# Attention loop of a block kernel: stack rows of maxima in halves, lead 18, six fixed score banks, split output copies

## The chip, the cores and the metric

The kernel runs on one core of a Trainium2 chip. A core has five engines with queues of their own: PE (TensorE, the matmuls, whose weight loads the profile lists apart as PEld), DVE (VectorE), ACT (ScalarE), POOL (GpSimd) and SP (SyncE, which issues most DMAs here). PE writes its results into PSUM, in banks of 128 partitions by 512 float32 values; DVE and ACT read them from there. Operands lie in SBUF, and what moves between SBUF and DRAM moves by DMA. The metric is the device time of one execution in microseconds (us), given as the median of several runs.

## The reference

The reference computes one block in float32 for S = 2048 tokens of width D = 640: attention over 32 heads of width 20 in which a token sees itself and the 255 tokens before it, then a gated MLP whose gate mixes tokens with a matrix of 2048 x 2048.

```python
def _A_ref(x, wqkv, wo):
    H = 32; Dh = D // H; W = 256
    q, k, v = ...                                   # x @ wqkv, by heads
    scores = jnp.einsum("bhqd,bhkd->bhqk", q, k) * (Dh ** -0.5)
    mask = (idx[:, None] - idx[None, :] >= 0) & (idx[:, None] - idx[None, :] < W)
    p = _softmax(jnp.where(mask, scores, -1e9), axis=-1)
    return jnp.einsum("bhqk,bhkd->bhqd", p, v).reshape(B, S, D) @ wo

def _B_ref(x, w_in, w_sp, b_sp, w_out):
    z = _gelu(jnp.einsum("bsd,df->bsf", x, w_in))
    z1, z2 = z[..., :Fh], _layernorm(z[..., Fh:], axis=-1)
    g = jnp.einsum("ts,bsf->btf", w_sp, z2) + b_sp[None, :, None]
    return jnp.einsum("bsf,fd->bsd", z1 * g, w_out)

h = x + _A_ref(_layernorm(x), A_wqkv, A_wo)
h2 = h + _B_ref(_layernorm(h), B_w_in, B_w_sp, B_b_sp, B_w_out)
```

## The kernel before

**Stages.** Up to some 85 us the kernel normalises x, transposes it and forms the values (turn1, vgemm). Then it forms queries and keys by 40 gemm items (qk_item), each of which is split into three bf16 parts (split_qk: ACT copies the first part, DVE takes the rest, ACT copies the second part, POOL takes the third) and stored to qk_d in DRAM. The last 16 of these items, cut into 80 steps of three matmuls by the generator dense_tail, are interleaved with the first maxima of the attention. From 249 to some 499 us the attention loop runs. The rest, to the end, is the output projection, the second layernorm and the MLP.

**Tiling of the attention.** There are eight groups of four heads and 16 key blocks of 128 tokens, in all NU = 128 units; a unit is one key block of one group. A stack of a group (a slot, of which three rotate: tiles slot0, slot1 and xb, each in two halves of 1024 tokens) holds the bf16 parts of queries and keys as rows 0 to 119, and as query rows 120 to 122 the negated maximum of each query in three bf16 parts. So the score matmul over 123 rows gives the score less its maximum, and ACT need only take the exponential. A stack is loaded by load_stack in DMAs on SP.

**One turn of the loop** (`for s in range(NU + 2)`) issues, four times, a maximum for unit s + LEAD and a score for unit s, and between them the two parts of the value product for unit s - 2:

- max_item: four column strips of 32 queries (L298; L302 in the prologue, where the tile is not cut into strips) into a PSUM bank, and a DVE operation (L307, "junk") that adds the mask and takes the maximum over keys into one column of mcol; its result comes out by an accumulator read, which the profile lists as an instruction of its own.
- score_item: four strips (L360) into a bank, then the exp on ACT (L362) into the tile pt, and after the fourth head one or two affine selects on POOL (L364, L367), which set masked values to zero.
- pv_item: the value products in float32 (L385) into PSUM, in the first part after the second score and in the second part after the fourth. After every fourth key block the sum goes to SBUF (tile ot, on ACT at L396 or DVE at L398) and to o_d by a DMA.
- max_rows, once per group, after the last maximum of a group: PE transposes mcol (L312), DVE splits the negated maxima into three bf16 parts (L315 to L319, tiles m3 and mr), one DMA stores them to m_d (L320) and two bring them into the rows 120 to 122 of the two halves of the stack (L323).

LEAD is 21. Before the loop, the prologue issues 16 units of group 0 with three gemm steps a unit, max_rows(0), and five units of group 1, of which the last has only its four maxima.

**PSUM.** Two banks are for the value products and the gemms (pv_tile). Three rotating tiles of one bank each are for maxima (s1_tile), and three fixed tiles of one bank each for scores (s2_tile); the layernorm stage uses s2_tile for the transposes of turn1 and s1_tile for the second half of vgemm. When the last unit's maxima are issued, at s = 107, the pool is opened again as three tiles of two banks, and the last 20 units are scored two heads at a time (width 2): unstripped, with one exp for both.

**What sets the order.** Up to the end of the attention the order on PE, DVE and ACT is the order in which the code emits the instructions; a planner places what SP and POOL do, and the work of the later stages. Which semaphore an instruction waits for is not written in the kernel: it is derived from the tiles that it reads and writes.

Of the kernel before, what the change touches and what calls it, by code (L numbers as in the profile page):

```python
# [7 lines left out]
F32 = mybir.dt.float32  # L8
# [26 lines left out]
def block_kernel(ctx, tc, x, wqk, wv, wo, w_in, wsp, bsp, w_out, out):  # L35
# [5 lines left out]
    def pool(stack, name, **kw):  # L41
        return stack.enter_context(tc.tile_pool(name=name, bufs=1, reuse_waits="tile", **kw))
# [156 lines left out]
    with ExitStack() as ab:  # L199
# [38 lines left out]
        psB = ab.enter_context(ExitStack())  # L238
        ps6 = [pool(psB, "ps6", space=PSUM)]
# [44 lines left out]
        def max_item(g, qb, hh, strips=True):  # L284

            st = slot_ap[g % 3]
            ps = s1_tile(f"sm{g}_{qb}_{hh}")
            lo = max(0, qb - 2) * P
            n = (qb + 1) * P - lo
            keep = mask[:, 384 - n:]  # L290
            if strips:
                skip = 32 if qb > 1 else 0
                if skip:
                    n, keep = 288, strip
                for j in range(4):
                    q0 = qb * P + 32 * j
                    for o, w, k in tokens(st, 120, 1, hh, lo + skip * j, n):
                        nc.tensor.matmul(ps[32 * j:32 * j + 32, o:o + w], one(st, 120, 0, hh, q0, 32), k,  # L298
                                         start=True, stop=True, tile_position=(0, 32 * j))
            else:  # L300
                for o, w, k in tokens(st, 120, 1, hh, lo, n):
                    nc.tensor.matmul(ps[:, o:o + w], one(st, 120, 0, hh, qb * P, P), k, start=True, stop=True)  # L302
            if qb == 0 and hh == 0:
                m_cols[g] = tmp2.tile([P, 64], F32, tag="mcol", bufs=2, name=f"mcol{g}")
            junk = tmp2.tile([P, 384], BF16, tag="junk", bufs=2, name=f"junk{g}_{qb}_{hh}")
            c = qb // 8 * 32 + hh * 8 + qb % 8
            nc.vector.tensor_tensor_reduce(out=junk[:, :n], in0=ps[:, :n], in1=keep, scale=1.0,  # L307
                                           scalar=NEG, op0=OP.add, op1=OP.max, accum_out=m_cols[g][:, c:c + 1])

        def max_rows(g):  # L310
            ps = s1_tile(f"mt{g}")
            nc.tensor.transpose(ps[:64, :P], m_cols.pop(g), ident)  # L312
            m3 = tmp2.tile([64, 3, P], BF16, tag="m3", bufs=1, name=f"m3_{g}")
            mr = tmp2.tile([64, P], F32, tag="mr", bufs=2, name=f"mr{g}")
            nc.vector.tensor_scalar(out=m3[:, 0], in0=ps[:64, :P], scalar1=-1.0, scalar2=None, op0=OP.mult)  # L315
            nc.vector.scalar_tensor_tensor(out=mr, in0=ps[:64, :P], scalar=-1.0, in1=m3[:, 0],
                                           op0=OP.mult, op1=OP.subtract)
            nc.vector.tensor_copy(out=m3[:, 1], in_=mr)
            nc.vector.tensor_tensor(out=m3[:, 2], in0=mr, in1=m3[:, 1], op=OP.subtract)  # L319
# [19 lines left out]
            yield  # L339


        def score_item(u, hh, width):
# [8 lines left out]
            if width == 1:  # L351
                ps = s2_tile(f"st{u}_{hh}")[:, None, :]
            else:
                ps = ps6[0].tile([P, 2, 512], F32, tag="sp", bufs=3, name=f"st{u}_{hh}")
            for j in range(width):
                for i in range(4):
                    k0 = kb * P + 32 * i
                    b, e = (32 * i, min(n, 32 * i + 288)) if width == 1 else (0, n)
                    for o, w, q in tokens(st, 123, 0, hh + j, kb * P + b, e - b):
                        nc.tensor.matmul(ps[32 * i:32 * i + 32, j, b + o:b + o + w], one(st, 123, 1, hh + j, k0, 32), q,  # L360
                                         start=True, stop=True, tile_position=(0, 32 * i))
            nc.scalar.activation(pt[:, hh:hh + width, :n], ps[:, :, :n], AF.Exp, scale=SCALE)  # L362
            if hh + width == 4:
                nc.gpsimd.affine_select(out=pt[:, :, :P], in_=pt[:, :, :P], pattern=[[0, 4], [1, P]], base=0,  # L364
                                        channel_multiplier=-1, compare_op=OP.is_ge, fill=0.0)
                if n == 384:
                    nc.gpsimd.affine_select(out=pt[:, :, 256:], in_=pt[:, :, 256:], pattern=[[0, 4], [-1, P]],  # L367
                                            base=-1, channel_multiplier=1, compare_op=OP.is_ge, fill=0.0)

        def pv_item(u):  # L370
# [20 lines left out]
            if kb % 4 == 3:  # L391
                c = kb // 4
                ps = pv_tiles.pop((g, c))
                ot = tmp3.tile([P, 512], F32, tag="ot", bufs=4, name=f"ot{g}_{c}")
                if u < NU - LEAD or u >= NU - 5:
                    nc.scalar.activation(ot, ps, AF.Copy)  # L396
                else:
                    nc.vector.tensor_copy(out=ot, in_=ps)  # L398
                nc.sync.dma_start(o_d[4 * g:4 * g + 4, :, c * 512:(c + 1) * 512].rearrange("h d t -> (h d) t"), ot)
                if g == 7:  # L400
                    inverse.append(inverse_sums(c))


        if True:
# [13 lines left out]
            def turn1(i):  # L418
                xn = xns.pop(i)
                c, o = divmod(i, 4)  # L420
                for k0, k1 in ((0, 4), (4, KD)):
                    ps = s2_tile(f"xt_ps{i}_{k0}")
# [8 lines left out]
            def vgemm(i):  # L431
                c, o = divmod(i, 4)
                t0 = o * P
                for j in range(2):
                    ps = (s1_tile if j else pv_tile)(f"v{i}_{j}")
# [145 lines left out]
        for s in range(NU + 2):  # L581
# [603 lines left out]
```

## Time and profile before

| | us |
|---|---|
| median of 3 runs | 1173.26 (1172.56 to 1174.24) |
| the profiled execution | 1168.04 |
| its span | 1166.4 |
| attention loop: first exp to last exp | 252.9 to some 491 |
| mean granted TensorE clock | 0.988 |

Busy time of the engines by stage (us; the last column is the granted clock):

| stage | span | PE | DVE | ACT | POOL | clock |
|---|---|---|---|---|---|---|
| layernorm, transposes, values, 0 to 85 | 85.0 | 76.2 | 42.9 | 31.5 | 22.0 | 1.00 |
| query and key gemms, 91 to 189 | 98.0 | 97.5 | 18.7 | 39.3 | 45.3 | 1.00 |
| gemms with maxima, 189 to 249 | 60.0 | 58.1 | 48.3 | 15.3 | 21.5 | 0.99 |
| attention loop, 249 to 500 | 251.0 | 225.0 | 204.6 | 210.4 | 157.2 | 0.97 |
| projection and MLP, 500 to the end | 666.4 | 638.0 | 434.4 | 240.1 | 145.7 | 0.99 |

In the profile's rows a line number is followed by the engine, the operation and the tiles, output before inputs, without buffer numbers. A share of busy time is a mean over the stretch that it is taken from. Successive matmuls overlap in the records, so a matmul's own duration is longer than its share of PE's order; the distance between starts tells the latter. In brackets at the end of a timeline row stands how long the engine was idle before, and what ended that.

### The profile page before, as it was taken

Reading aid. Unit: us, or ns where it says so; the run is one execution under the profiler, and the core shown is the slowest. Engines: PE = TensorE matmul, PEld = TensorE weight load, DVE = VectorE, ACT = ScalarE, POOL = GpSimd, SP = SyncE. Lnnn points to the kernel's source line nnn. Section 1 sums busy time; section 2 is a strip of 40 time slices with the busy share of each in tenths; the row PEclk is TensorE's granted clock in tenths of the full one; section 3 lists DMA queues with packets and bytes.
Section 4 is the critical chain, followed back from the end, with each engine's and each line's share of the span. In section 5 each row is a group of like instructions: output and inputs, shape, how many; then the busy total and the mean of one; then the engine's idle time right before and its main releaser. Section 6 shows DMA issues by size and latency. Waiting matters only on the chain. (4 is left out here: it accounts for less than half of the span.)

```text
span 1166.4 us, 28287 instructions
## 1 busy us (share of the span) xinstructions
PE 1100.8 (94%) x11084; PEld 983.9 (84%) x11084; DVE 748.8 (64%) x1950; ACT 538.5 (46%) x1122; POOL 394.0 (34%) x480
## 2 busy tenths in 40 slices
PE   6999999989898999888999998999999899999998
PEld 6998877657777776577999997899999799999998
DVE  5541214878888895679858579655548984655443
ACT  4334433248888898634346544433334431222110
POOL 3124443436565666756412055000116430000000
PEclk9999999989999999999999999999999999999999
DMA  6212454654445523567745511233341454444322
GB/s 205 68 40 86 160 188 148 223 188 162 162 168 168 174 94 99 197 210 263 257 151 207 176 66 55 78 113 112 118 140 63 141 184 136 142 134 141 91 84 79
DMA packets 75061, 165.32 MB, mean 142 GB/s; under 512 B 10112, under 2 KB 34432, under 8 KB 71040
## 3 DMA queue, kind: packets, MB, share of 16 engines
q1 hardware_dynamic: 72624, 158.28, 40.6%
q10 hardware_dynamic: 2304, 5.24, 1.2%
q8 instruction: 87, 1.43, 0.5%
q14 instruction: 46, 0.38, 0.1%
HBM read 108.83 MB, written 54.66 MB: 140 GB/s over the span
## 5 line engine op out<-in xcount | busy, mean ns | idle before, releaser
L362 ACT ACTIVATE pt<-s 128x384 f32<-128x384 f32 (+2 forms) x432 | 171.8, 496 | 22.2 <-PE sm L298 13.7
L650 ACT ACTIVATE aw<-fx 128x512 fp32r<-128x512 f32 (+2 forms) x160 | 92.9, 596 | 188.9 <-PE g L982 121.9
L982 PE MATMUL g<-zl,aw 128*128 128x432 f32 x768 | 172.6, 360 | 7.4 <-ACT zl L650 4.9
L307 DVE CUSTOM_DVE_ANT_0 junk<-sm,strip 128x288 bf16<-128x288 f32 x380 | 153.9, 454 | 20.6 <-PE sm L298 17.1
L982 PEld LDWEIGHTS g<-zl,aw 128*128 128x128 f32 x768 | 143.9, 188 | 15.2 <-ACT zl L650 5.7
L982 PE MATMUL g<-ze,aw 128*128 128x432 f32 x576 | 137.0, 365 | 5.3 <-DVE row L644 3.1
L644 DVE TENSOR_TENSOR aw<-fx,aw 128x512 fp32r<-128x512 f32 (+2 forms) x152 | 109.8, 730 | 36.0 <-ACT aw L650 31.2
L385 PE MATMUL pv<-pt,v_sb 128*32 128x192 f32 (+3 forms) x1984 | 128.7, 323 | 4.2 <-POOL pt L364 2.5
L982 PEld LDWEIGHTS g<-ze,aw 128*128 128x128 f32 x576 | 108.9, 192 | 12.7 <-DVE row L644 2.8
L364 POOL TENSOR_SCALAR_AFFINE_SELECT pt<-pt 128x512 f32<-128x512 f32 x128 | 85.5, 668 | 82.4 <-ACT pt L362 82.2
L1021 PE MATMUL out_ps<-wout,y_sp 128*128 128x320 f32 (+1 forms) x630 | 96.4, 309 | 0.5 <-ACT y_sp L122 0.4
L360 PE MATMUL s<-slot 123*32 123x288 bf16 (+5 forms) x1216 | 88.7, 280 | 8.1 <-DMA slot<-m_d 4.2
L1021 PEld LDWEIGHTS out_ps<-wout,y_sp 128*128 128x128 f32 (+1 forms) x630 | 94.1, 188 | 1.5 <-ACT y_sp L122 0.7
L886 PE MATMUL zb<-win,aw 128*128 128x432 f32 x480 | 95.3, 359 | 0.0
L886 PEld LDWEIGHTS zb<-win,aw 128*128 128x128 f32 x480 | 90.0, 187 | 4.7
L298 PE MATMUL sm<-slot 120*32 120x288 bf16 (+8 forms) x1200 | 86.5, 280 | 2.2 <-DVE mcol L307 1.6
L480 DVE TENSOR_TENSOR rest<-qk,sg 128x512 f32<-128x512 f32 x40 | 27.7, 691 | 86.5 <-ACT sg L478 86.5
L360 PEld LDWEIGHTS <-slot 123*32 123x32 bf16 x1728 | 59.3, 97 | 25.6 <-issue 8.5
L483 POOL TENSOR_TENSOR sg<-rest,sg 128x512 bf16<-128x512 f32 x40 | 46.6, 1165 | 81.2 <-ACT sg L482 77.1
L367 POOL TENSOR_SCALAR_AFFINE_SELECT pt<-pt 128x512 f32<-128x512 f32 x112 | 72.9, 651 | 0.0
L385 PEld LDWEIGHTS pv<-pt,v_sb 128*32 128x32 f32 x1984 | 59.7, 110 | 14.0 <-POOL pt L364 6.7
L644 DVE TENSOR_TENSOR row<-g,row 128x432 f32<-128x432 f32 x80 | 47.9, 603 | 35.7 <-PE g L982 32.8
(181 smaller groups left out, 2245.0 us busy)
## 6 DMA issues: line engine op xcount, KB each, us to landing
slot<-qk_d SPq DMA_DIRECT2D x144, 160.0 KB
fx<-wsp_in SPq DMA_DIRECT2D x32, 512.0 KB
qk_d<-sg SPq DMA_DIRECT2D x40, 384.0 KB
fx<-hn_d SPq DMA_DIRECT2D x32, 320.0 KB
o_d<-ot SPq DMA_DIRECT2D x32, 256.0 KB
xb<-qk_d SPq DMA_DIRECT2D x48, 160.0 KB
z_d<-row SPq DMA_DIRECT2D x16, 432.0 KB
g_d<-row SPq DMA_DIRECT2D x16, 432.0 KB
```

The lines of the kernel that those rows point to most:

```text
L298: nc.tensor.matmul(ps[32 * j:32 * j + 32, o:o + w], one(st, 120, 0, hh, q0, 32), k, start=True, stop=True, tile_position=(0, 32 * j))
L307: nc.vector.tensor_tensor_reduce(out=junk[:, :n], in0=ps[:, :n], in1=keep, scale=1.0, scalar=NEG, op0=OP.add, op1=OP.max, accum_out=m_cols ...
L360: nc.tensor.matmul(ps[32 * i:32 * i + 32, j, b + o:b + o + w], one(st, 123, 1, hh + j, k0, 32), q, start=True, stop=True, tile_position=(0 ...
L362: nc.scalar.activation(pt[:, hh:hh + width, :n], ps[:, :, :n], AF.Exp, scale=SCALE)
L364: nc.gpsimd.affine_select(out=pt[:, :, :P], in_=pt[:, :, :P], pattern=[[0, 4], [1, P]], base=0, channel_multiplier=-1, compare_op=OP.is_ge ...
L367: nc.gpsimd.affine_select(out=pt[:, :, 256:], in_=pt[:, :, 256:], pattern=[[0, 4], [-1, P]], base=-1, channel_multiplier=1, compare_op=OP. ...
L385: nc.tensor.matmul(ps[32 * hh:32 * hh + 32, a - 512 * c:b - 512 * c], v_sb[:, kb, v0:v0 + 32], pt[:, hh, a - kb * P:b - kb * P], start=fir ...
L644: (eng or nc.vector).tensor_tensor(out=out, in0=a, in1=b, op=op)
L650: nc.scalar.activation(out, a, AF.Copy)
L886: nc.tensor.matmul(b[0][:, :HF], a[t][:, x, kk], win2[0][:, y, kk, h * HF:(h + 1) * HF], start=kk + x + y == 0, stop=kk == KD - 1 and x == 1)
L982: nc.tensor.matmul(ps, w[m][:, x, k], zc[k][m][:, y], start=start and k + x + y == 0, stop=stop and k == 3 and x == 1, skip_group_check=True)
L1021: nc.tensor.matmul(ps[j][:, :HD], src[:w, a, k, :], e1["wout"][:w, b, k, j * HD:(j + 1) * HD], start=(k == 0 and a + b == 0), stop=(k == K ...
```

## The change

Five things change together.

1. **PSUM.** Six banks serve maxima and scores from the first stage to the end of the attention: three tiles of two banks each, wide0 to wide2. The ring for maxima (and the values' second half) is made of the second bank of wide1 and both banks of wide2, the ring for scores (and turn1) of both banks of wide0 and the first bank of wide1. When the last maxima are issued, one bank goes over from the first ring to the second. No pool is opened again; all scores are done one head at a time, in strips.
2. **Rows of maxima.** max_rows runs for each half of a group, eight query blocks, so 16 times on 32 rows in place of 8 times on 64. The second and third part are formed on POOL in place of DVE; m3 has two buffers. A store and a load serve each half.
3. **LEAD** is 18.
4. **Prologue.** 18 units with gemm steps among them: three a unit for the first 12, then four.
5. **Output copies.** Up to unit 109 ACT copies columns 0 to 255 of ot and DVE columns 256 to 511; then DVE copies all up to unit 122, and ACT from there.

```diff
-    m_d = dram.tile([8, 3, 64, 64], F32, name="m_d")
+    m_d = dram.tile([8, 2, 3, 32, 64], F32, name="m_d")
...
-        LEAD = 21
+        LEAD = 18
...
-        s2s, s2n = [ps6[0].tile([P, 512], F32, name=f"s2_{i}") for i in range(3)], [0]
-        def s1_tile(name):
-            return ps6[0].tile([P, 512], F32, tag="s1", bufs=3, name=name)
-        def s2_tile(name):
-            s2n[0] += 1
-            return s2s[s2n[0] % 3]
+        ps6 = pool(ab, "ps6", space=PSUM)
+        wide = [ps6.tile([P, 2, 512], F32, name=f"wide{i}") for i in range(3)]
+        banks = [w[:, i] for w in wide for i in range(2)]
+        ring = {1: banks[3:], 2: banks[:3]}
+        def s_tile(which):
+            ring[which].append(ring[which].pop(0))
+            return ring[which][-1]
+        def s1_tile():
+            return s_tile(1)
+        def s2_tile():
+            return s_tile(2)
...
-        def max_rows(g):
-            ps = s1_tile(f"mt{g}")
-            nc.tensor.transpose(ps[:64, :P], m_cols.pop(g), ident)
...
+        def max_rows(g, b):
+            ps = s1_tile()[:32, :P]
+            nc.tensor.transpose(ps, m_cols.pop((g, b)), ident)
+            m3 = tmp2.tile([32, 3, P], BF16, tag="m3", bufs=2, name=f"m3_{g}_{b}")
...
-            nc.vector.tensor_copy(out=m3[:, 1], in_=mr)
-            nc.vector.tensor_tensor(out=m3[:, 2], in0=mr, in1=m3[:, 1], op=OP.subtract)
-            nc.sync.dma_start(m_d[g].rearrange("a r c -> r a c"), m3.bitcast(F32))
-            st = slot_w[g % 3]
-            for b in range(2):
-                nc.sync.dma_start(st[b][120:123, 0],
-                                  m_d[g][:, 32 * b:32 * b + 32].rearrange("a (h r) c -> a h (r c)", h=4))
+            nc.gpsimd.tensor_copy(out=m3[:, 1], in_=mr)
+            nc.gpsimd.tensor_tensor(out=m3[:, 2], in0=mr, in1=m3[:, 1], op=OP.subtract)
+            rows = m_d[g, b]
+            nc.sync.dma_start(rows.rearrange("a r c -> r a c"), m3.bitcast(F32))
+            nc.sync.dma_start(slot_w[g % 3][b][120:123, 0], rows.rearrange("a (h r) c -> a h (r c)", h=4))
...
-            nc.scalar.activation(pt[:, hh:hh + width, :n], ps[:, :, :n], AF.Exp, scale=SCALE)
+            nc.scalar.activation(pt[:, hh, :n], ps[:, :n], AF.Exp, scale=SCALE)
...
-                if u < NU - LEAD or u >= NU - 5:
-                    nc.scalar.activation(ot, ps, AF.Copy)
-                else:
-                    nc.vector.tensor_copy(out=ot, in_=ps)
+                mid = 256 if u < NU - LEAD else 0 if u < NU - 5 else 512
+                if mid:
+                    nc.scalar.activation(ot[:, :mid], ps[:, :mid], AF.Copy)
+                if mid < 512:
+                    nc.vector.tensor_copy(out=ot[:, mid:], in_=ps[:, mid:])
...
-            for u in range(16):
+            for u in range(LEAD):
                 for hh in range(4):
-                    max_item(0, u, hh, False)
-                    if hh < 3:
+                    max_item(u // NT, u % NT, hh, False)
+                    if hh or u >= 12:
                         next(dense, None)
-            max_rows(0)
-            for u in range(LEAD - 16):
-                for hh in range(4):
-                    if u:
-                        max_item(1, u - 1, hh, False)
-                    next(dense, None)
-            for hh in range(4):
-                max_item(1, LEAD - 17, hh, False)
+                if u % 8 == 7:
+                    max_rows(u // NT, u % NT // 8)
...
-                if s <= NU - LEAD:
-                    score_item(s, hh, 1)
-                elif s < NU and hh % 2 == 0:
-                    score_item(s, hh, 2)
-                if hh == 3 and u1 % NT == 0 and u1 <= NU:
-                    max_rows(u1 // NT - 1)
+                if s < NU:
+                    score_item(s, hh)
+                if hh == 3 and u1 % 8 == 0 and u1 <= NU:
+                    max_rows((u1 - 8) // NT, (u1 - 8) % NT // 8)
                 if hh == 2 + s - NU and s >= NU:
-                    pre_ps.append(proj_o(s - NU, ps6[0].tile([P, 2, 512], F32, tag="sp", bufs=3,
-                                                             name=f"wo_ps{s - NU}")))
+                    pre_ps.append(proj_o(s - NU, wide[2 * (NU + 1 - s)]))
...
             if u1 == NU:
-                psB.close()
-                ps6[0] = pool(psB, "ps6t", space=PSUM)
+                ring[2].append(ring[1].pop(0))
```

More of the change, by code (lines that the diff above doesn't have):

```diff
@@ L233, in block_kernel @@
         nc.gpsimd.memset(v4[:, :, :, 20:21], 1.0)
-        LEAD = 21
+        LEAD = 18
         NU = 128
-        psB = ab.enter_context(ExitStack())
-        ps6 = [pool(psB, "ps6", space=PSUM)]
-        s2s, s2n = [ps6[0].tile([P, 512], F32, name=f"s2_{i}") for i in range(3)], [0]
-        def s1_tile(name):
-            return ps6[0].tile([P, 512], F32, tag="s1", bufs=3, name=name)
-        def s2_tile(name):
-            s2n[0] += 1
-            return s2s[s2n[0] % 3]
+        ps6 = pool(ab, "ps6", space=PSUM)
[9 more added lines that the diff above has]
+            return s_tile(2)
         def pv_tile(name):
@@ L286, in max_item @@
             st = slot_ap[g % 3]
-            ps = s1_tile(f"sm{g}_{qb}_{hh}")
+            ps = s1_tile()
             lo = max(0, qb - 2) * P
@@ L302, in max_item @@
                     nc.tensor.matmul(ps[:, o:o + w], one(st, 120, 0, hh, qb * P, P), k, start=True, stop=True)
-            if qb == 0 and hh == 0:
-                m_cols[g] = tmp2.tile([P, 64], F32, tag="mcol", bufs=2, name=f"mcol{g}")
+            b, c = divmod(qb, 8)
+            if c == 0 and hh == 0:
+                m_cols[g, b] = tmp2.tile([P, 32], F32, tag="mcol", bufs=2, name=f"mcol{g}_{b}")
             junk = tmp2.tile([P, 384], BF16, tag="junk", bufs=2, name=f"junk{g}_{qb}_{hh}")
-            c = qb // 8 * 32 + hh * 8 + qb % 8
+            c += hh * 8
@@ L307, in max_item @@
             nc.vector.tensor_tensor_reduce(out=junk[:, :n], in0=ps[:, :n], in1=keep, scale=1.0,
-                                           scalar=NEG, op0=OP.add, op1=OP.max, accum_out=m_cols[g][:, c:c + 1])
-        def max_rows(g):
-            ps = s1_tile(f"mt{g}")
-            nc.tensor.transpose(ps[:64, :P], m_cols.pop(g), ident)
[L313 to L316, printed above, removed]
-                                           op0=OP.mult, op1=OP.subtract)
-            nc.vector.tensor_copy(out=m3[:, 1], in_=mr)
-            nc.vector.tensor_tensor(out=m3[:, 2], in0=mr, in1=m3[:, 1], op=OP.subtract)
-            nc.sync.dma_start(m_d[g].rearrange("a r c -> r a c"), m3.bitcast(F32))
-            st = slot_w[g % 3]
-            for b in range(2):
-                nc.sync.dma_start(st[b][120:123, 0],
-                                  m_d[g][:, 32 * b:32 * b + 32].rearrange("a (h r) c -> a h (r c)", h=4))
@@ new lines, in max_item @@
+                                           scalar=NEG, op0=OP.add, op1=OP.max, accum_out=m_cols[g, b][:, c:c + 1])
+        def max_rows(g, b):
+            ps = s1_tile()[:32, :P]
+            nc.tensor.transpose(ps, m_cols.pop((g, b)), ident)
+            m3 = tmp2.tile([32, 3, P], BF16, tag="m3", bufs=2, name=f"m3_{g}_{b}")
+            mr = tmp2.tile([32, P], F32, tag="mr", bufs=2, name=f"mr{g}_{b}")
+            nc.vector.tensor_scalar(out=m3[:, 0], in0=ps, scalar1=-1.0, scalar2=None, op0=OP.mult)
+            nc.vector.scalar_tensor_tensor(out=mr, in0=ps, scalar=-1.0, in1=m3[:, 0],
+                                           op0=OP.mult, op1=OP.subtract)
+            nc.gpsimd.tensor_copy(out=m3[:, 1], in_=mr)
[3 more added lines that the diff above has]
+            nc.sync.dma_start(slot_w[g % 3][b][120:123, 0], rows.rearrange("a (h r) c -> a h (r c)", h=4))
@@ L339, in inverse_sums, with score_item @@
             yield
-        def score_item(u, hh, width):
+        def score_item(u, hh):
             g, kb = divmod(u, NT)
@@ L350, in score_item @@
             pt = p_tiles[u]
-            if width == 1:
-                ps = s2_tile(f"st{u}_{hh}")[:, None, :]
-            else:
[L354 to L363, printed above, removed]
+            ps = s2_tile()
+            for i in range(4):
+                k0 = kb * P + 32 * i
+                b, e = 32 * i, min(n, 32 * i + 288)
+                for o, w, q in tokens(st, 123, 0, hh, kb * P + b, e - b):
+                    nc.tensor.matmul(ps[32 * i:32 * i + 32, b + o:b + o + w], one(st, 123, 1, hh, k0, 32), q,
+                                     start=True, stop=True, tile_position=(0, 32 * i))
+            nc.scalar.activation(pt[:, hh, :n], ps[:, :n], AF.Exp, scale=SCALE)
+            if hh == 3:
                 nc.gpsimd.affine_select(out=pt[:, :, :P], in_=pt[:, :, :P], pattern=[[0, 4], [1, P]], base=0,
@@ L421, in turn1 @@
                 for k0, k1 in ((0, 4), (4, KD)):
-                    ps = s2_tile(f"xt_ps{i}_{k0}")
+                    ps = s2_tile()
                     for k in range(k0, k1):
@@ L434, in vgemm @@
                 for j in range(2):
-                    ps = (s1_tile if j else pv_tile)(f"v{i}_{j}")
+                    ps = s1_tile() if j else pv_tile(f"v{i}_{j}")
                     n0 = j * HD
```

1 line of the change is left out of this document (removed).

## The prediction

> **What bounds the kernel now.** I read the page's engine shares first, then a table of windows over the attention loop, then the waits of that stretch, then single stretches of the timeline, because the change touches only the stretch up to 499 us and each stage has its own limit. First the share of busy time, then windows (span in us; busy time and count for PE, weight loads, DVE, ACT, POOL; clock, DMA share, GB/s):
>
> ```profile
> PE 1100.8 (94%) x11084; PEld 983.9 (84%) x11084; DVE 748.8 (64%) x1950; ACT 538.5 (46%) x1122; POOL 394.0 (34%) x480
> ```
>
> ```profile
> 25.00:50.00 25.00, 25.00 (x179) 24.98 (x178) 13.09 (x33) 8.22 (x20) 3.96 (x10) 1.00 0.26 80
> 244.50:248.00 3.50, 2.24 (x9) 0.67 (x7) 3.50 (x15) 0.37 (x1) 1.61 (x1) 0.99 0.74 209
> 248.00:251.40 3.40, 2.95 (x31) 1.08 (x30) 3.37 (x14) 0.42 (x1) 0.00 (x0) 0.50 0.59 224
> 309.40:312.80 3.40, 1.69 (x59) 1.25 (x48) 2.19 (x12) 1.27 (x6) 1.39 (x3) 1.00 0.07 17
> 405.79:433.67 27.88, 27.04 (x833) 22.59 (x829) 26.07 (x131) 26.53 (x69) 18.17 (x30) 1.00 0.34 113
> ```
>
> The last row is one undisturbed group of 16 units: 1.74 us a unit, PE busy for 97%, DVE for 94% and ACT for 95%. Three engines are within 6% of each other, so any lost overlap shows at once. The waits between 249 and 455 us (total, times, longest) show how little PE waits for the readers of its score banks now, and that the stack rows are late by 9 us in all:
>
> ```profile
> PE s L360 <- DMA xb<-m_d: 4.8, 2, 3.0
> PE s L360 <- DMA slot<-m_d: 4.2, 3, 1.6
> PE s L360 <- ACT pt L362: 3.8, 7, 1.7
> PE sm L298 <- DVE mcol L307: 2.2, 7, 0.3
> ```
>
> The price of one hand-over between PE and its readers is in the timeline (start, duration):
>
> ```profile
> 252.93 2.02 ACT L362 ACTIVATE pt<-s 128x384 f32<-128x384 f32 x5 [1.32 <-POOL sg L483]
> 253.47 0.43 PE L360 MATMUL s<-slot 123*32 123x288 bf16 x4 [1.66 <-ACT pt L362]
> 253.66 0.48 PE L298 MATMUL sm<-slot 120*32 120x288 bf16 x4
> 254.19 0.46 DVE L307 CUSTOM_DVE_ANT_0 junk<-sm,strip 128x288 bf16<-128x288 f32 x1 [1.74 <-PE sm L298]
> 286.94 0.51 PE L385 MATMUL pv<-pt,v_sb 128*32 128x192 f32 x8
> 287.26 0.31 PE L298 MATMUL sm<-xb 120*32 120x288 bf16 x4
> 287.39 0.31 PE L360 MATMUL s<-slot 123*32 123x288 bf16 x4
> 287.62 0.46 DVE L307 CUSTOM_DVE_ANT_0 junk<-sm,strip 128x288 bf16<-128x288 f32 x1 [0.40 <-PE sm L298]
> 288.00 0.08 DVE L307 DVE_READ_ACCUMULATOR2_ANT mcol<- 128x1 f32 x1
> 337.10 0.07 DVE L307 DVE_READ_ACCUMULATOR2_ANT mcol<- 128x1 f32 x1
> 337.23 0.29 PE L298 MATMUL sm<-slot 120*32 120x256 bf16 x4 [0.32 <-DVE mcol L307]
> 337.33 0.31 PE L360 MATMUL s<-xb 123*32 123x288 bf16 x4
> 337.69 1.81 ACT L362 ACTIVATE pt<-s 128x384 f32<-128x384 f32 x4 [0.25 <-PE s L360]
> ```
>
> An item of four strips takes 0.13 us of PE's order (287.26 to 287.39), a part of the value product 0.32 (286.94 to 287.26). From a maximum's start to its reduction's start 0.36 passes (287.26 to 287.62), the reduction with its accumulator read takes 0.46 (to 288.08), and a PE item that waits for it starts 0.06 later (337.17 to 337.23): 0.88 in all. From a score to its exp 0.36 (337.33 to 337.69), from the exp's start to a PE item that waits for it 0.54 (252.93 to 253.47): 0.90. Exps follow each other at 0.41 (2.02/5).
>
> **The change part by part.** What decides is how the six fixed banks are kept apart. The built program tells: dependences are held per tile, and a tile now has two banks. Before, 435 of 440 scores in the loop wait for the exp three back and 410 maxima for the reduction three back; a maximum waits for DVE alone and a score for ACT alone. After, of 440 scores 146 wait for the exp directly before, 102 for the one two back and 103 for the reduction of a maximum; of 440 maxima 138 wait for the reduction directly before, 89 for two back, and 97 for an exp one or two back. Two neighbours of the built order, both in wide1, whose first half is for scores and second for maxima:
>
> ```
> 2207 L301 Matmult wide1_115<-slot1_1_1917 32x288 [waits Activation_49]
> 2233 L359 Matmult wide1_115<-slot0_1_98 32x288 [waits DVE_49]
> ```
>
> Maxima use banks 1b, 2a, 2b in turn, scores 0a, 0b, 1a. Each max_rows takes one bank of the first ring, so every 8 units the pairing moves by one, through three phases of equal length. I follow three pairs (maximum, score) of each.
>
> Phase A, pairs 1b/1a, 2a/0a, 2b/0b: maximum 1b at 0, score 1a waits for its reduction to 0.88; maximum 2a at 1.01, score 0a at 1.14, its exp behind that of 1a at 1.65; score 0b waits for it to 2.19; next pair at 2.32. Phase B, 1b/0a, 2a/0b, 2b/1a: score 0a at 0.13, 0b behind its exp at 1.03, 1a at 1.28, whose exp queues behind that of 0b and starts at 1.80; maximum 1b waits for it: 2.34. Phase C, 2b/0a, 1b/0b, 2a/1a: score 0b at 1.03, maximum 2a at 1.16, and 2b waits for its reduction: 2.04. Value products (1.5 parts in three pairs, 0.48) are covered in part; I add half, 0.24, in A and 0.15 in B and C. Mean (2.56 + 2.49 + 2.19)/3 = 2.41; a unit has four pairs: 3.2 us against 1.74.
>
> The loop's first 110 units: 110 x 3.2 = 352. In 14 of them (key blocks 14 and 15) tiles are narrower: -7.
>
> Output copies. The rows of this and of the next parts, by tile and form (count: shortest/mean/longest ns, first to last start), then one wait:
>
> ```profile
> L315 DVE TENSOR_SCALAR m<-mt x8: 282/283/284, 234.9 to 453.8; 64x128 bf16<-64x128 f32 x8
> L316 DVE SCALAR_TENSOR_TENSOR mr<-mt,m x8: 282/282/283, 235.2 to 454.1; 64x128 f32<-64x128 f32 x8
> L319 DVE TENSOR_TENSOR m<-mr,m x8: 284/603/603, 235.8 to 454.7; 64x128 bf16<-64x128 f32 x8
> L362 ACT ACTIVATE pt<-s x432: 271/492/618, 252.9 to 453.7; 128x384 f32<-128x384 f32 x128, 128x256 f32<-128x256 f32 x8, 128x128 f32<-128x128 f32 x8
> L362 ACT ACTIVATE pt<-st x40: 365/811/934, 454.7 to 490.8; 128x768 f32<-128x768 f32 x32, 128x512 f32<-128x512 f32 x4, 128x256 f32<-128x256 f32 x4
> L396 ACT ACTIVATE ot<-pv x28: 598/628/652, 263.9 to 498.6; 128x512 f32<-128x512 f32 x28
> L398 DVE COPY ot<-pv x4: 622/691/693, 456.2 to 480.2; 128x512 f32<-128x512 f32 x4
> L428 ACT ACTIVATE xa<-s x16: 269/426/599, 8.0 to 43.5; 128x512 fp32r<-128x512 f32 x8, 128x128 fp32r<-128x128 f32 x8
> L429 DVE TENSOR_TENSOR xa<-s,xa x16: 281/483/693, 8.6 to 44.3; 128x512 fp32r<-128x512 f32 x8, 128x128 fp32r<-128x128 f32 x8
> ```
>
> ```profile
> ACT osp L154 <- DVE m L146: 3.9, 1, 3.9
> ```
>
> ```profile
> ACT osp L154 <- DVE m L146: 3.9, 1, 3.9
> ```
>
> A half takes about half of 0.63 on ACT and of 0.69 on DVE, and DVE's half waits for ACT's, being in one tile. Behind it in DVE's queue stands the next reduction, for which PE now waits. 27 copies; each between 0 (it falls where DVE idles) and 0.66 (both halves in series on the path). I take 0.4, nearer the upper end since A and B leave little slack: +11.
>
> Rows of maxima. 14 calls in the loop in place of 7; 13 maxima wait for the second DVE operation after the transpose, 0.30 of PE (estimate from the 0.28 of its neighbours) + 0.28 + 0.28: 14 x 0.9 = +12. The two operations moved to POOL cost between 0.6 each (L319, DVE) and 1.15 (POOL, 251.74 below, a larger tile), lie beside POOL's idle time (18.17 of 27.88 busy) and delay only the stores. One store and one load per half go out on SP in place of one store and two loads per group: 32 transfers in place of 24. Rows are now needed 8 units after their issue, or 10, some 26 us, before 5 units, 8.7 us: the 9 us of DMA waits above go. With the loop bound by hand-overs they are inside the 3.2. If this cover failed, the old 9 us would come back. On SP the store waits for POOL's last operation; behind it stand loads of a stack, needed a group later, and output stores, whose tiles have four buffers: no one on the path waits for them.
>
> Loop: 352 - 7 + 11 + 12 = 368 for 110 units; before, 108 units (432 exps) took 202 (first exp 252.93, first wide one 454.7). Two more units leave the tail. **Loop +166.**
>
> Start of the loop and prologue:
>
> ```profile
> 243.20 0.28 PE L302 MATMUL sm<-slot 120*128 120x256 bf16 x1
> 243.79 0.40 PE L466 MATMUL qk<-xb,wql 128*128 128x512 f32 x1
> 244.03 0.66 PE L302 MATMUL sm<-slot 120*128 120x384 bf16 x3
> 245.02 0.32 PE L302 MATMUL sm<-slot 120*128 120x384 bf16 x1 [0.33 <-DVE mcol L307]
> 250.98 0.63 ACT L482 ACTIVATE sg<-rest 128x512 bf16<-128x512 f32 x1 [6.11 <-DVE rest L480]
> 251.74 1.15 POOL L483 TENSOR_TENSOR sg<-rest,sg 128x512 bf16<-128x512 f32 x1 [5.63 <-ACT sg L482]
> ```
>
> The last gemm step ends at 244.2 (243.79 + 0.40), then twelve bare maxima keep DVE before the last split, and the first exp starts at 252.93: 8.7. After, no maxima trail, and the split's chain is some 0.6 (L478's copy, taken as L482's) + 0.69 + 0.63 + 1.15 = 3.1: **-5.5**. In the prologue 24 of 72 maxima (2b after 2a) wait for the reduction directly before: 0.99 (244.03 to 245.02) less 0.83 (maximum and step, 243.20 to 244.03) = 0.17 for 20, and 0.83 for four without a step between: **+7**.
>
> Layernorm stage: the second transpose of a block waits for ACT's and DVE's split of the first, 0.60 + 0.69 = 1.29. PE is full in 25 to 50 us, where six of the sixteen lie: **+8**; bounds 0 and 16 x 1.29 = 21.
>
> Tail: exps singly, four banks, two of them one tile: 0.90 + 3 x 0.41 = 2.13 a unit, 18 x 2.13 = 38, and the 3.9 that ACT stands behind a normalisation, 42; before 36.1 (454.7 to 490.8) for 20 units: **+6**.
>
> Sum: 166 - 5.5 + 7 + 8 + 6 = +181.5. The profiled execution took 1168.04, so 1349.5; the median of the runs is 5.2 above it: **1355**.
>
> **The rivals.**
> Clock: PE would be busy 8 x 0.13 + 2 x 0.32 = 1.68 of 3.2 us, 52%. Below full clock were the 3.4 us after a window with 2.24 of 3.50 busy (244.50, 9 matmuls); a window with 1.69 of 3.40 busy (309.40, 59 matmuls) kept 1.00 in itself. So the trace leaves it open. At clock 0.50 a maximum is 0.53 from its reduction (253.66 to 254.19) and items are 0.19 apart: three latencies and three pairs of items longer by 0.17 and 0.12, value products doubled, together some +0.9 to +1.1 in 2.41, so +1.2 to +1.4 a unit: +45 for a third of the loop, 1400; +140 for all, 1495.
> The Trainium skill, page "TensorE: Matmul & The Clock Gate", section "A second HAM failure mode: psum-queue depth-cycling", says that cycling through PSUM banks can idle PE often enough that its clock swings between half and full; no row of before shows such swinging in the loop, whose groups stand at 1.00, and by it the time would be this rival's.
> Milder: waits overlap better than I followed them, all phases run like C with the products hidden, 2.04 x 4/3 = 2.7 a unit: 352 becomes 297, in all 1300. For it: latencies are single rows. Against: 284 waits are on the item directly before.
> The other side: the two halves are in effect separate (the waits fall on readers long done). Then the loop keeps 1.74 to 1.89 a unit, the 9 us of row waits and 5.5 at the start go, ACT gains some 0.3 x 27 = 8 and the tail loses 4: about 1155. It decides if waits cost under 0.15 us a unit; the hand-over rows speak against it, with 0.9 where a wait is on the neighbour.
>
> **How the numbers follow.** Serial hand-overs at full clock 0.60, own range 1315 to 1390 from the bounds of copies, stage and value products; clock 0.23; milder 0.12; other side 0.05. 1355 is the likeliest. Range 1285 to 1455: above it lies a third of the clock case, below it the other side and part of the milder. A difference within 0.2% (2.3 us) is about what can't be told from no change; faster 0.04, same 0.01, slower 0.95.
>
> **What would show it.** Right: units 3.2 us apart in the loop, PE near 50% there, waits of scores for the reduction (L311) and the exp (L361) and of maxima for both, hundreds each; waits for the stack rows gone; first exp about 3 us after the last gemm step; a wait of the copy on DVE for ACT's. Wrong: units still 1.7 to 1.9 apart, or a clock of 0.5 over whole groups.

## The result, and the profile after

The changed kernel takes 1379.88 us (median of 5 runs, 1376.97 to 1380.78) against 1172.56 (median of 5, 1171.0 to 1174.24): ratio 1.1765, 95% interval 1.1745 to 1.1784. The forecast was 1355, in a range of 1285 to 1455. The profiled execution took 1376.97 us with a span of 1375.1, so 208.7 more than the span of before. Cut at the same events, the 208.7 lie so (us; the loop has 108 units with maxima or single exps before, 110 after):

| stretch | before | after | more | forecast |
|---|---|---|---|---|
| to the first query gemm | 91.3 | 103.2 | +11.9 | +8 |
| query and key gemms with the first maxima | 152.9 | 160.7 | +7.8 | +7 |
| last gemm step to first exp | 8.7 | 3.4 | -5.3 | -5.5 |
| loop | 201.8 | 384.8 | +183.0 | +166 |
| tail, to the last exp | 36.1 | 43.6 | +7.5 | +6 |
| to the end | 675.6 | 679.3 | +3.7 | 0 |

The first cuts are read from the first and last starts of the gemms' rows, before and after:

```profile
L464 PE MATMUL qk<-xa,wqh x100: 392/396/531, 91.3 to 206.5; 128*128 128x512 f32 x100
```

```profile
L464 PE MATMUL qk<-xa,wqh x100: 389/396/531, 103.2 to 222.3; 128*128 128x512 f32 x100
L466 PE MATMUL qk<-xb,wql x100: 388/389/398, 110.7 to 263.5; 128*128 128x512 f32 x100
```

The page's busy shares of after show no engine that has become the bound: PE fell from 94% of the span to 86%, with nearly the same matmuls.

```profile
PE 1183.6 (86%) x11128; PEld 993.7 (72%) x11128; DVE 775.8 (56%) x1976; ACT 571.1 (42%) x1163; POOL 397.3 (29%) x512
PEclk9999999889899799989989999999999999999999
```

What the loop waits for stands in the waits of after between 264 and 652 us (total, times, longest). Each of the four hand-overs between PE and the readers of its banks is there, where before had 3.8 us for the exps and 2.2 for the reductions; the waits for stack rows are gone.

```profile
PE wide L359 <- DVE mcol L311: 44.9, 67, 1.7
PE wide L359 <- ACT pt L361: 25.1, 67, 1.2
PE wide L301 <- DVE mcol L311: 24.2, 62, 0.5
PE wide L301 <- ACT pt L361: 18.2, 41, 0.6
DVE junk L311 <- ACT pt L361: 31.8, 56, 1.5
DVE ot L398 <- ACT ot L396: 14.5, 27, 0.9
```

One such hand-over in the timeline of after: a maximum (519.52), its reduction (519.98) and accumulator read (to 520.44), and only then, 0.98 us after the maximum, the score, which goes into the other bank of the same tile. The reduction starts 0.46 us after its maximum, 0.10 later than in the row that priced the hand-over. The view puts such a wait down to an exp (56 times in the loop, 31.8 us); before has none, and the forecast has no term for it:

```profile
519.52 0.33 PE L301 MATMUL wide<-xb 120*32 120x288 bf16 x4
519.67 0.08 DVE L311 DVE_READ_ACCUMULATOR2_ANT mcol<- 128x1 f32 x1
519.98 0.46 DVE L311 CUSTOM_DVE_ANT_0 junk<-wide,strip 128x288 bf16<-128x288 f32 x1 [0.23 <-ACT pt L361]
520.36 0.08 DVE L311 DVE_READ_ACCUMULATOR2_ANT mcol<- 128x1 f32 x1
520.50 0.31 PE L359 MATMUL wide<-slot 123*32 123x288 bf16 x4 [0.65 <-DVE mcol L311]
```

The loop by eights of units, from one set of rows to the next (windows of after; columns as in the prediction, the granted clock third from the end), six of the twelve whole ones:

```profile
374.56:399.22 24.66, 18.45 (x385) 10.83 (x378) 14.53 (x66) 14.79 (x34) 8.41 (x15) 0.93 0.32 106
399.22:426.80 27.58, 18.69 (x437) 11.60 (x437) 15.54 (x69) 16.07 (x34) 10.45 (x19) 1.00 0.28 94
426.80:460.73 33.93, 22.89 (x395) 13.37 (x398) 15.79 (x71) 14.65 (x35) 10.09 (x18) 0.71 0.23 79
543.89:567.82 23.93, 17.28 (x385) 10.36 (x378) 14.47 (x66) 14.78 (x34) 8.41 (x15) 1.00 0.33 108
567.82:595.36 27.54, 18.68 (x437) 11.61 (x437) 15.52 (x69) 16.06 (x34) 10.44 (x19) 1.00 0.07 23
595.36:627.38 32.02, 20.03 (x401) 12.09 (x404) 15.69 (x72) 14.53 (x34) 10.09 (x18) 0.84 0.06 21
```

The three phases come in turn: 3.0, 3.4 and 3.9 or more us a unit (C, B and A of the prediction, by the order of the rings), and the clock falls mostly in the slowest. With the units cut at the starts of their first exps, 90 of the 110 ran at full clock (a mean above 0.97 over the unit), 3.31 us each; the other 20 at a mean clock of 0.63, 4.35 each. (The expectation of e6_max_twice below has 3.30, 4.26 and 0.69: there the clock of a unit was put together from windows of 3.41 us, which counts 87 and 23.) But 18 of these 20 units are of phase A, which takes 3.7 us at full clock as it is. Against the full-clock mean of its own phase the low clock cost about 14 us of the loop (an estimate), and the rest, some 370, is the waits'.

### The profile page after: what moved, and what is told of

It reads as the page before. It is cut to its first block, busy times and chain, and to the rows that moved or that the text cites. A ratio compares the mean times of both kernels' runs of the same rounds, so it can differ in the third digit from the quotient of the medians.

```text
span 1375.1 us, 28570 instructions
## 1 busy us (share of the span) xinstructions
PE 1183.6 (86%) x11128; PEld 993.7 (72%) x11128; DVE 775.8 (56%) x1976; ACT 571.1 (42%) x1163; POOL 397.3 (29%) x512
## 5 line engine op out<-in xcount | busy, mean ns | idle before, releaser
L361 ACT ACTIVATE pt<-wide 128x384 f32<-128x384 f32 (+2 forms) x512 | 232.3, 471 | 183.0 <-PE wide L359 156.0
L311 DVE CUSTOM_DVE_ANT_0 junk<-wide,strip 128x288 bf16<-128x288 f32 x392 | 175.3, 456 | 141.8 <-PE wide L301 101.2
L359 PE MATMUL wide<-slot 123*32 123x288 bf16 (+8 forms) x1536 | 116.4, 297 | 74.5 <-DVE mcol L311 39.8
L363 POOL TENSOR_SCALAR_AFFINE_SELECT pt<-pt 128x512 f32<-128x512 f32 x128 | 82.2, 642 | 263.0 <-ACT pt L361 260.8
L359 PEld LDWEIGHTS <-slot 123*32 123x32 bf16 x1728 | 64.3, 99 | 122.2 <-issue 112.6
L384 PE MATMUL pv<-pt,v_sb 128*32 128x192 f32 (+3 forms) x1984 | 136.0, 346 | 0.0
L301 PE MATMUL wide<-slot 120*32 120x288 bf16 (+3 forms) x1248 | 97.4, 296 | 27.5 <-DVE mcol L311 16.8
L301 PEld LDWEIGHTS <-slot 120*32 120x32 bf16 x1408 | 52.8, 99 | 67.5 <-issue 57.9
L366 POOL TENSOR_SCALAR_AFFINE_SELECT pt<-pt 128x512 f32<-128x512 f32 x112 | 72.2, 645 | 0.0
L311 DVE CUSTOM_DVE_ANT_0 junk<-wide,mask 128x384 bf16<-128x384 f32 (+2 forms) x120 | 52.6, 449 | 32.7 <-PE wide L305 18.1
```

The costliest lines, as they stand in the source:

```text
L359: nc.tensor.matmul(ps[32 * i:32 * i + 32, b + o:b + o + w], one(st, 123, 1, hh, k0, 32), q, start=True, stop=True, tile_position=(0, 32 * i))
L361: nc.scalar.activation(pt[:, hh, :n], ps[:, :n], AF.Exp, scale=SCALE)
L384: nc.tensor.matmul(ps[32 * hh:32 * hh + 32, a - 512 * c:b - 512 * c], v_sb[:, kb, v0:v0 + 32], pt[:, hh, a - kb * P:b - kb * P], start=fir ...
```

## The experiments

**The banks undone, and the banks alone.** e1_six_tiles makes the six banks six tiles; e2_before_wide gives the kernel before the three shared tiles and the rings, and nothing else of the change. In e1 the pool is opened again at the very end, for the projection's tiles of two banks. Their edits:

```diff
...
-        wide = [ps6.tile([P, 2, 512], F32, name=f"wide{i}") for i in range(3)]
-        banks = [w[:, i] for w in wide for i in range(2)]
+        banks = [ps6.tile([P, 512], F32, name=f"bank{i}") for i in range(6)]
...
+                if s == NU and hh == 0:
+                    psB.close()
+                    ps6 = pool(psB, "ps6t", space=PSUM)
+                    wide = [ps6.tile([P, 2, 512], F32, name=f"wide{i}") for i in range(3)]
```

```diff
-        s2s, s2n = [ps6[0].tile([P, 512], F32, name=f"s2_{i}") for i in range(3)], [0]
+        wide = [ps6[0].tile([P, 2, 512], F32, name=f"wide{i}") for i in range(3)]
+        banks = [w[:, i] for w in wide for i in range(2)]
+        ring = {1: banks[3:], 2: banks[:3]}
+        def s1_tile(name):
+            return s_tile(1)
+        def s2_tile(name):
+            return s_tile(2)
```

> The changed kernel with one edit: the six score banks are six tiles of one bank each in place of three tiles of two; rings, lead 18, rows of maxima in halves, split copies, prologue and single exps stay. In the built program 437 of 440 scores of the loop now wait for the exp three back and 401 of 440 maxima for the reduction three back. Theory (the shared tiles cause the loss): the loop goes back to some 1.8 to 1.9 us a unit at a granted clock near 1.00, the first query gemm starts near 91 us again, and the time is the 1168 us of before less 5 us at the start of the loop and up to 9 us of waits for stack rows, give or take the copies: 1150 to 1165 us. Rival A (lead, halves of rows, split copies or single exps carry the loss): above 1250 us. Rival B (the low clock in the loop carries it and has a cause other than the waits): units stay at 1.9 us or less only at full clock, with windows of 0.50 as in the changed kernel, some 1190 us.

> The kernel before with one part of the change alone: maxima and scores use the two rings over three tiles of two banks; lead 21, whole output copies on ACT, one set of rows per group, the old prologue and the two-head tail stay. Theory: the shared tiles alone bring nearly all of it: first gemm about 12 us later, units of the loop 3.2 us at full clock, low clock in a fifth of the windows for another 20 us: 168 + 1180 = about 1350 us (1320 to 1380). Rival A (the other parts carry the loss): below 1250 us.

Measured: e1 1165.39 us (ratio to before 0.9946, interval 0.9926 to 0.9967), at the upper edge of what I expected; e2 1362.6 us (one run). In e2 the four hand-overs are there, in its waits between 249 and 650 us:

```profile
PE wide L365 <- DVE mcol L312: 33.5, 53, 1.6
PE wide L365 <- ACT pt L367: 29.4, 82, 0.8
PE wide L303 <- ACT pt L367: 26.5, 52, 2.4
PE wide L303 <- DVE mcol L312: 23.3, 54, 1.5
```

In e1 the same 110 units take 204.5 us, 1.86 each. Its eights alternate between 1.77 and 1.87 to 2.16; two of them, in the windows of e1:

```profile
396.42:410.61 14.19, 12.86 (x394) 10.68 (x389) 13.03 (x68) 12.52 (x35) 9.25 (x16) 1.00 0.59 186
410.61:425.56 14.95, 14.11 (x448) 12.12 (x439) 13.69 (x68) 13.72 (x35) 10.42 (x18) 1.00 0.23 82
```

The shared tiles are the cause of the loss: without them the rest of the change is 0.5% faster than before (rival A falls, and B too, as the clock of the loop is 0.99 again); with them alone the kernel loses 192 us. The first query gemm of e1 starts at 91.8, so all but 0.5 of the 11.9 us of the layernorm stage are theirs as well.

**The output copies**, with the banks apart (e3_six_copy_act, on top of e1) and with them shared (e8_after_copy_act, on the changed kernel). The edit is one line in both:

```diff
-                mid = 256 if u < NU - LEAD else 0 if u < NU - 5 else 512
+                mid = 512 if u < NU - LEAD or u >= NU - 5 else 0
```

> Six tiles of one bank as in the first run, and the output copies whole on ACT for units before 110 again (DVE whole for 110 to 122), in place of the two halves. Theory: with the banks apart, the loop is bound by PE, DVE and ACT within 6% of each other; a half on DVE costs 27 x (0.43 + wait for ACT's half) and saves 27 x 0.25 on ACT, so whole copies change the time by -10 to +7 us against the first run. If the half on DVE was a real cost of the change even with banks apart, this run is over 5 us faster than the first; if it was a gain, over 5 us slower.

> The changed kernel with whole output copies on ACT for units before 110 (DVE whole for 110 to 122), so that no reduction stands behind a DVE half that waits for ACT's half. It prices the split with the shared tiles in place. Theory: the prediction's term, 27 x 0.4 = 11 us, less what 0.25 more of ACT per copy costs on the path (0 to 7): 1366 to 1376 us. Rival (the split is hidden in the loop's idle time): within 3 us of the changed kernel's 1377 to 1381; or slower, up to 1387, if ACT's 0.25 falls on the path.

Measured: e3 1152.98 us (ratio 0.9849, 0.981 to 0.9887), 12.4 less than e1; e8 1368.84 us (ratio 1.1698, 1.1647 to 1.1749), 11 less than the changed kernel, with intervals that just touch. With the banks apart the split is a loss, outside the -10 that I gave as the end. In the waits of e1 over the whole run the cost stands as DVE's wait for the other half:

```profile
DVE ot L398 <- ACT ot L396: 14.1, 27, 0.8
```

In the profiled execution of e8 the full-clock units take 3.29 us as against 3.31 and the loop 384.2 as against 384.8, so the loop shows nothing of it. But that execution is the longest of e8's four (1375.73 us at a mean clock of 0.961); the other three took 1366.18 to 1369.01 at 0.966 to 0.975, where the changed kernel's five had 0.959 to 0.967. So e8's 11 us go with a higher granted clock, and what raised it no trace here shows.

**The tail** (e4_six_wide_tail, on top of e1):

```diff
...
-                if s < NU:
-                    score_item(s, hh)
+                if s <= NU - LEAD:
+                    score_item(s, hh, 1)
+                elif s < NU and hh % 2 == 0:
+                    score_item(s, hh, 2)
...
-                ring[2].append(ring[1].pop(0))
+                psB.close()
+                ps6[0] = pool(psB, "ps6t", space=PSUM)
```

> Six tiles of one bank as in the first run, and the tail of before: at the last maxima the pool is opened again as three tiles of two banks and the last units are scored two heads at a time with one exp. Theory: in the first run the tail of single exps with four separate banks runs at ACT's 0.41 us an exp, 1.7 us a unit with its copies, against 0.81 us for two heads; so the two differ by less than 3 us either way. If single exps are a cost of the change (as its 7.6 us longer tail suggests), this run is 3 to 8 us faster than the first.

Measured: 1164.66 us against 1165.39 of e1, no difference. Single exps cost nothing by themselves; the longer tail of the changed kernel is that of two banks in one tile (e1 takes 29.2 us for the same 18 units, from 454.7 to 483.9, the changed kernel 43.6).

**Another pairing** (e5_pair_each, on the changed kernel), which asks whether the price of each wait is understood:

```diff
-        ring = {1: banks[3:], 2: banks[:3]}
+        ring = {1: banks[1::2], 2: banks[::2]}
```

> The changed kernel with one edit: each of the three shared tiles gives its first bank to the scores' ring and its second to the maxima's. In the built program 431 of 440 scores now wait for the reduction of a maximum, and 426 of 440 maxima for an exp one, two or three back; no score waits for another exp. Theory (each wait costs the hand-over read from the timeline): three phases again, by how far the rings stand apart: in step, a score waits for the maximum just before it, 0.88 + 0.13 a pair, 4.0 us a unit and 4.3 with the value products; one bank apart, a score waits for the maximum of the pair before and the pair takes 0.51, 2.1 to 2.4 a unit; two apart, a maximum waits for the exp just before it, 0.90 + 0.13 a pair, 4.1 to 4.4 a unit. So, by eights of units at full clock, two slow eights and a fast one in turn, mean 3.7 and 3.85 with copies and rows: 1377 + 110 x 0.55 = about 1435 us (1400 to 1470). Rival (sharing costs some fixed amount whatever the pairing): eights of 3.0 to 3.7 as in the changed kernel, 1365 to 1390 us.

Measured: 1498.26 us, above the range. Three eights of its loop:

```profile
617.37:653.84 36.47, 25.47 (x385) 13.67 (x381) 15.91 (x70) 15.02 (x35) 10.01 (x18) 0.62 0.22 71
653.84:706.52 52.68, 32.21 (x445) 16.96 (x445) 16.19 (x71) 16.24 (x34) 10.83 (x19) 0.50 0.04 12
706.52:731.97 25.45, 20.29 (x389) 11.80 (x389) 14.19 (x65) 14.78 (x34) 8.16 (x15) 0.84 0.07 24
```

Two slow eights and a fast one in turn, as forecast, and the pairing does matter (4.6, 6.6 and 3.2 us a unit here): the rival falls. Two sizes were off: the fast units at full clock take 2.9, not 2.1 to 2.4, and the loop's mean clock is 0.64, which the forecast left at 1.00. The slow units can hardly be compared. Thirteen units of the slow eights ran at full clock, all where a fast eight goes over into a slow one: seven of them take 3.0 to 3.8, the other six 4.1 to 4.5, where I had 4.1 to 4.4. The second slow eight of each turn never ran at full clock.

**What holds the clock down** (e6_max_twice, on the changed kernel): more PE work, the same waits.

```diff
-                        nc.tensor.matmul(ps[32 * j:32 * j + 32, o:o + w], one(st, 120, 0, hh, q0, 32), k,
-                                         start=True, stop=True, tile_position=(0, 32 * j))
+                        for _ in range(2):
+                            nc.tensor.matmul(ps[32 * j:32 * j + 32, o:o + w], one(st, 120, 0, hh, q0, 32), k,
+                                             start=True, stop=True, tile_position=(0, 32 * j))
```

> The changed kernel with the four strips of each maximum in the loop issued twice into the same bank (the second time over the first), which adds PE work and changes no wait. It tells what holds the clock down in the loop: windows at a mean clock of 0.92, units of 3.30 us at full clock and 4.26 at 0.69. Theory (the clock falls because PE is busy too little of the time): PE's share rises, fewer than a third as many of the loop's windows are below full clock, and the loop's mean clock is 0.97 or more; each maximum takes 0.13 longer on the path, up to 0.5 us a unit: 1377 - 22 + 30 to 55 = 1385 to 1410 us. Rival (the hand-overs themselves, the swinging between banks, bring it down): the mean clock of the loop stays at 0.90 to 0.94, and the time is 1410 to 1435 us.

Measured: 1402.88 us, in the range; the loop's mean clock is 0.98, and 107 of 110 units ran at full clock, 3.73 us each. Three of its eights, the same units as the last three quoted of after:

```profile
563.95:590.31 26.36, 20.42 (x523) 14.06 (x514) 14.59 (x66) 14.85 (x34) 8.39 (x15) 1.00 0.30 99
590.31:621.19 30.88, 22.75 (x601) 15.46 (x590) 15.75 (x69) 16.24 (x34) 10.48 (x19) 1.00 0.07 21
621.19:653.42 32.23, 20.12 (x533) 14.43 (x536) 15.63 (x71) 14.53 (x35) 10.02 (x18) 1.00 0.06 21
```

The clock comes back although every hand-over is still there and a unit has got 0.37 us longer (at full clock, phase against phase): it is too little PE work per time that brings it down, not the changing of banks.

**The rows alone** (e9_before_halves, on the kernel before; max_rows as in the change, called at u = 7 and 15 of the prologue and here):

```diff
-                if hh == 3 and u1 % NT == 0 and u1 <= NU:
-                    max_rows(u1 // NT - 1)
+                if hh == 3 and u1 % 8 == 0 and u1 <= NU:
+                    max_rows((u1 - 8) // NT, (u1 - 8) % NT // 8)
```

> The kernel before with one part of the change alone: stack rows in halves of eight query blocks (16 transposes, third parts on POOL, a store and a load for each half), at lead 21. Theory: rows come eight units earlier relative to their use, so the 9 us of waits for stack rows and most of what follows them go (up to 12), against eight more transposes with two DVE operations of 0.28 each, 0.9 each if PE and DVE wait for it, 7 in all: 1160 to 1170 us where the kernel before has 1171. Rival (the transposes cost more than the waits): 1172 to 1180 us.

Measured: 1159.15 us (ratio 0.9902, 0.9878 to 0.9927), 12.9 less than before and 1 below the range: the waits for stack rows go, and the added transposes cost so little where the banks are apart that no run here resolves it.

The best kernel of these is e3, 1.5% faster than before: the change with its banks as six tiles and whole copies.

## Why the prediction was right, and where it was off

Right in cause and in place. Dependences held per tile, read from the built order, were the cause: e1 and e2 show it from both sides.

- **The three phases.** The hand-over prices gave 3.41, 3.32 and 2.92 us a unit for A, B and C, and 0.15 on top for copies and rows. At full clock the eights take 3.7, 3.4 and 3.0; the mean with all terms was forecast at 368/110 = 3.35 and came out at some 370/110 = 3.36. What A takes beyond its 3.41 and the 0.15 may be the later reductions (0.10 in one of three pairs, 0.13 a unit, an estimate); that is not shown. Two counts of the sum were off by 1 us each, in opposite directions: 12 of the 110 units are narrower, not 14, and 13 calls of max_rows fall among them, not 14.
- **The clock.** Here the likeliest case failed: it kept the loop at full clock and made the low one a rival of 0.23 that excludes it. The run has both. The low clock took 20 units of 110 and about 14 us, half of the 27 by which the sum fell short of the 208.7. The row that I weighed, PE busy 1.69 of 3.40 us at clock 1.00, was a single window; the loop offers a hundred, and some have less in them. Two places where the clock fell (at 441.08 and 608.34), in windows of after that are cut there, and then one stretch of e1 that kept it:

```profile
437.67:441.08 3.41, 1.62 (x39) 0.80 (x29) 1.91 (x8) 1.65 (x5) 0.91 (x2) 1.00 0.58 190
441.08:444.49 3.41, 2.42 (x38) 1.45 (x39) 1.43 (x7) 1.58 (x4) 0.82 (x2) 0.50 0.61 210
604.92:608.34 3.42, 1.63 (x48) 1.01 (x37) 1.73 (x7) 1.75 (x5) 1.22 (x2) 1.00 0.00 0
608.34:611.75 3.41, 2.33 (x40) 1.24 (x32) 1.40 (x6) 1.81 (x4) 1.22 (x2) 0.50 0.21 77
```

```profile
321.94:325.35 3.41, 1.59 (x70) 1.38 (x60) 1.66 (x8) 1.32 (x4) 1.62 (x4) 1.00 0.69 256
325.35:328.76 3.41, 3.31 (x100) 2.87 (x94) 3.20 (x17) 3.14 (x9) 2.36 (x4) 1.00 0.44 117
```

  After 1.62 and 1.63 us of PE in 3.41, the clock is at 0.50. With the changed kernel's loop cut into such stretches, seven at full clock were followed by a fall, and PE's records cover 47 to 56% of them; of those that kept it one has 52% and all others 57% or more. The share alone does not decide, since e1 went on at full clock after 1.59 us in 3.41. The Trainium skill, page "TensorE: Matmul & The Clock Gate", section "A second HAM failure mode: psum-queue depth-cycling", says that PE idling between bursts on cycled banks makes the clock swing; the trace agrees, with 0.50 to 1.00 in the loop, and e6 shows that it is the idling.
- **Copies.** The term of 11 us is 12.4 where the banks are apart, which is in part luck, as it was worked out for the shared tiles. In the changed kernel's profiled loop it does not show at full clock, so there that part of the sum stays unproven, and what A took over its 3.41 stood in its place. A half takes 0.38 us on ACT and 0.42 on DVE, more than the halves of 0.63 and 0.69 that I had. That DVE's half waits because both are in one tile is not shown either: both halves also read the same bank.
- **Layernorm stage.** 11.9 (11.4 of it the shared tiles') in place of 8: between the bounds of 0 and 21, mis-sized because I counted only the six blocks at which PE was full for certain.
- **Prologue and start of the loop.** -5.3 for -5.5, as worked out. 7.8 for 7 is in part luck: e1, with the banks apart, takes 155.0 us for the same stretch, 2.1 more than before, so the waits' part is 5.7.
- **Tail.** 7.5 for 6. Units take 2.04 us there, as against 2.13; but the normalisation that the planner put ahead of the exps holds ACT for 6.3 us, not 3.9, since DVE's part of it stands 7.8 us behind the DMA of the inverse sums, and PE's next scores stand behind ACT (timeline of after):

```profile
686.57 1.56 DVE L146 TENSOR_TENSOR m<-m 128x640 f32<-128x640 f32 x2 [7.80 <-DMA inv<-o_d]
687.42 0.74 ACT L154 ACTIVATE osp<-m 128x640 fp32r<-128x640 f32 x1 [6.30 <-DVE m L146]
688.97 0.67 PE L359 MATMUL wide<-slot 123*32 123x288 bf16 x8 [7.44 <-ACT pt L361]
```

- **After the loop.** +3.7 us was in no term, and I have not found its cause. From the last exp to the end the eight experiments take 673.1 to 678.7 us, before 675.6 and after 679.3, so little of it stands clear of their spread.
- **Rows.** The 9 us of waits for stack rows went, as forecast; e9 gives the part's own worth, 12.9 us, which the change hides under its loss. Of the +12 for the transposes the waits of after show 3.5 us directly (PE for the second DVE operation, L321, 12 times); the rest can't be told apart.

## What to carry to other kernels

Before reading a change of buffers for its depth, read whose readers each write will wait for: six banks are six buffers only if the dependences are kept for each of them, and two banks of one tile are one buffer with two tenants. When engines that were 95% busy side by side fall into series, price the loop by its hand-overs (about 0.9 us each here), phase by phase, and then look at the TensorE clock, since a PE with half its time idle can also lose its speed. A bundle of edits can hide a good one: the rows in halves are worth 1% and the whole bundle cost 18%.

## What was not expected of the hardware

- The granted clock can rest at 0.50 for a whole stretch: 52.68 us in e5 (653.84 to 706.52), though PE's records cover 32.21 of them, 61%. In the changed kernel 47% (1.62 of 3.41) at full clock came before a fall. Records grow longer as the clock falls (four strips of a maximum 0.48 us at 0.50 in the row of 253.66, 0.31 at 1.00 in that of 287.26), so busy shares at different clocks are not to be compared.
- More PE work on the path was partly paid back by the clock: in e6 units at full clock grew by 0.37 us, some 40 for 110 (an estimate, phase against phase), but the loop grew by only 29 (384.8 to 413.5).
